# Attention in groups of two head pairs, with the transposes of the next group ahead of the scores of this one, on one Trainium2 core

## The chip, the cores and the metric

The kernel runs on one core of a Trainium2 chip. A core has engines that work side by side, each through its own list of instructions, in order: TensorE (PE in the profile; its weight loads are PEld), VectorE (DVE), ScalarE (ACT), GpSimd (POOL) and SyncE (SP), which here only issues transfers. 16 DMA engines move data between the chip's memory (HBM), the on-chip SBUF and PSUM, the small memory into which matmuls write. The metric is the device time of one execution in microseconds (us), as the median of several runs.

## The reference

Two stages follow each other. In the first, attention for B = 8 batches, H = 8 heads, S = 576 positions and D = 64, with two kinds of mask:

```
rel        = pos[:, None] - pos[None, :]
mask_plain = (rel >= 0) & (rel < 32)                       # heads 0 to 3
mask_dil   = (rel >= 0) & (rel < 128) & (rel % 4 == 0)     # heads 4 to 7
scores = where(mask, (q @ k.T) / sqrt(D), -1e9)
attn   = softmax(scores);   attn_out = attn @ v
```

In the second, the heads of a position are put side by side, so that x has 8 x 576 = 4608 rows of 8 x 64 = 512, and a feed-forward layer follows:

```
x = attn_out.transpose(0, 2, 1, 3).reshape(4608, 512)
h = x @ w_in             # 512 x 2048
g = h * sigmoid(h)
out = g @ w_out          # 2048 x 512
```

Inputs and output are float32.

## The kernel before, in words

**Set-up.** GpSimd builds the two masks as 128 x 512 tiles (L70 to L106), and its DMA queue then loads both weight matrices and casts them to bf16 on the way (L112, L113). Both masks reach at most 127 positions back, so a tile of 128 keys meets only the queries of its own tile and of the next one, 256 in all.

**A batch (loop at L180).** 576 positions are four tiles of 128 and a tail of 64. q and k are loaded by SP's queue and v by GpSimd's, a tile at a time (L184 to L195), then cast to bf16 on DVE into qb, kb and vb (L199 to L210). vb has two extra columns of ones per head, so that the matmul with v also gives the sum of the softmax. The load tiles qn, kn, vn and the cast tiles qb, kb, vb each have two buffers.

**A head pair (loop at L216), four to a batch.** Two heads fill the 128 partitions together:

1. Five PE transposes bring q of the pair into a PSUM tile `tpsq`, five bring k into `tpsk` (L227). DVE copies the first to qTp (L233), ACT the second to kTp (L235). qTp and kTp have two fixed buffers, used in turn. The trace calls both PSUM tiles tps, and the buffers of kTp kTp_307 and kTp_308.
2. For each of five key tiles j: two score matmuls (L241, L248), one for each head of the pair, into a PSUM tile sps; exp on ACT into Ej (L258); then DVE multiplies Ej by the mask in place (L259).
3. For each of the two heads: nine PV matmuls into the PSUM tile O_all (L274, L283, L291), a copy to SBUF, ost, on ACT (L301), then on DVE the reciprocal of the sums (L304) and the normalising product into xstage (L305, L312).

After the fourth pair SP issues two transfers of the batch's xstage to the DRAM tile x_sc (L321, L328).

**Buffers.** [...]transposes of q and of k one bank each (`T_psum`, one buffer for each), scores 2 buffers of two banks each (`S_psum`), PV results 2 buffers (`O_psum`). Ej has three buffers for each j. 

**Feed-forward (L139 to L174).** Nine blocks of 512 positions. Each loads x_sc with a DMA transpose (L142, SP), then one PE pass of 64 matmuls makes h (L149), with the sigmoid on ACT (L157) and the product on DVE (L158), and one more pass of 64 matmuls makes the output (L164), which ACT copies out of PSUM (L172) and SP stores (L174).

**What sets the order.** A tile scheduler puts the instructions of each engine in a list when the kernel is built. It gives priority by the order in which the program writes the operations, takes what it thinks ready by its own estimates of duration, and adds semaphore waits where an operation needs another's data or a buffer that is still in use. On the chip each engine goes through its list in order: an instruction that waits holds everything behind it on that engine.

The lines where a batch starts its pairs and fetches its buffers are short:

```
for hp in range(H // 2):
    ...
    qTc = qTp[hp % 2]
    kTc = kTp[hp % 2]
```

Of the kernel before, what the change touches and what calls it, by code (L numbers as in the profile page):

```python
# [9 lines left out]
ACT = mybir.ActivationFunctionType  # L10
ALU = mybir.AluOpType

NEG_BIAS = -3.0e4

PROBE = {"phase2": True, "scores": True, "pv": True, "norm": True, "xsc_write": True, "transposes": True}


@with_exitstack
def kernel(
# [9 lines left out]
    nc = tc.nc  # L29
    B, H, S, D = q.shape  # L30
# [3 lines left out]
    scale = 1.0 / math.sqrt(D)  # L34
# [3 lines left out]
    P = 128  # L38
    f32 = mybir.dt.float32
    bf16 = mybir.dt.bfloat16  # L40

    n_full_c = S // P
    tail = S - n_full_c * P
    n_qt = n_full_c + (1 if tail > 0 else 0)
    QT_W = (n_qt + 1) * P
# [9 lines left out]
    qkT_sb = cx1.enter_context(tc.tile_pool(name="qkT_sb", bufs=1))  # L55
    epool = cx1.enter_context(tc.tile_pool(name="e_pool", bufs=3))
    xst = cx1.enter_context(tc.tile_pool(name="xstage", bufs=2))
    rpool = cx1.enter_context(tc.tile_pool(name="r_pool", bufs=2))
    opool = cx1.enter_context(tc.tile_pool(name="o_pool", bufs=2))
    T_psum = cx1.enter_context(tc.tile_pool(name="T_psum", bufs=1, space=bass.MemoryType.PSUM))  # L60
    S_psum = cx1.enter_context(tc.tile_pool(name="S_psum", bufs=2, space=bass.MemoryType.PSUM))
    O_psum = cx1.enter_context(tc.tile_pool(name="O_psum", bufs=2, space=bass.MemoryType.PSUM))
# [37 lines left out]
    mask_pair = []  # L100
# [11 lines left out]
    nc.gpsimd.dma_start(out=w_in_bf, in_=moe_w_in.rearrange("(o p) f -> p o f", p=P))  # L112
    nc.gpsimd.dma_start(out=w_out_bf, in_=moe_w_out.rearrange("(o p) f -> p o f", p=P))  # L113

    qTp = [qkT_sb.tile([P, QT_W], bf16, name=f"qTp{i}") for i in range(2)]
    kTp = [qkT_sb.tile([P, S], bf16, name=f"kTp{i}") for i in range(2)]
    for t in qTp:
        nc.vector.memset(t[:, S:QT_W], 0.0)

    TB = 512  # L120
    n_blk = n_tok // TB
    n_nblk = d_ff // P
# [54 lines left out]
        moe_block_span(p * TB, TB)  # L177

    blocks_done = 0
    for b in range(B):  # L180
        qn = ld_nat.tile([P, n_qt, H, D], f32, tag="qn")
        kn = ld_nat.tile([P, n_qt, H, D], f32, tag="kn")
        vn = ld_nat.tile([P, n_qt, H, D], f32, tag="vn")
# [24 lines left out]
                out=vb[0:tail, n_full_c, :, 0:D], in_=vn[0:tail, n_full_c, :, :]  # L208
            )
        nc.vector.memset(vb[:, :, :, D : D + 2], 1.0)  # L210

        xstage = xst.tile([P, n_qt, H, D], bf16, tag="xstage")
        if not (PROBE["scores"] and PROBE["pv"] and PROBE["norm"]):
            nc.vector.memset(xstage[:, :, :, :], 0.0)

        for hp in range(H // 2):  # L216
            hA = 2 * hp
            mtile = mask_pair[0] if hA < H // 2 else mask_pair[1]

            qTc = qTp[hp % 2]  # L220
            kTc = kTp[hp % 2]
            if PROBE["transposes"]:
                for src, dstT, tagT in ((qb, qTc, "tpsq"), (kb, kTc, "tpsk")):
                    tps = T_psum.tile([P, S], bf16, tag=tagT)
                    for c in range(n_qt):
                        tn = P if c < n_full_c else tail
                        nc.tensor.transpose(  # L227
                            tps[:, c * P : c * P + tn],
                            src[0:tn, c, hA : hA + 2, :],
                            ident_bf[0:tn, 0:tn],  # L230
                        )
                    if src is qb:
                        nc.vector.tensor_copy(out=dstT[:, 0:S], in_=tps[:, 0:S])  # L233
                    else:
                        nc.scalar.copy(out=dstT[:, 0:S], in_=tps[:, 0:S])  # L235

            E = []
            for j in (range(n_qt) if PROBE["scores"] else ()):
                kn_j = P if j < n_full_c else tail
                sps = S_psum.tile([P, 8 * P], f32, tag="sps2")  # L240
                nc.tensor.matmul(  # L241
                    sps[0:kn_j, 0 : 2 * P],
                    lhsT=kTc[0:D, P * j : P * j + kn_j],
                    rhs=qTc[0:D, P * j : P * j + 2 * P],
                    start=True,
                    stop=True,
                )
                nc.tensor.matmul(  # L248
                    sps[0:kn_j, 4 * P : 6 * P],
                    lhsT=kTc[D : 2 * D, P * j : P * j + kn_j],  # L250
                    rhs=qTc[D : 2 * D, P * j : P * j + 2 * P],
                    start=True,
                    stop=True,
                )
                Ej = epool.tile([P, 4 * P], bf16, tag=f"E{j}")
                sps_view = sps[0:kn_j, :].rearrange("k (a b) -> k a b", b=4 * P)[:, :, 0 : 2 * P]
                e_view = Ej[0:kn_j, :].rearrange("k (a b) -> k a b", b=2 * P)
                nc.scalar.activation(out=e_view, in_=sps_view, func=ACT.Exp, scale=scale)  # L258
                nc.vector.tensor_tensor(  # L259
                    out=Ej[0:kn_j, :], in0=Ej[0:kn_j, :], in1=mtile[0:kn_j, :], op=ALU.mult  # L260
                )
                E.append((Ej, kn_j))

            for hh in (range(2) if (PROBE["pv"] and E) else ()):
                h = hA + hh
                oh = 2 * P * hh
                O_all = O_psum.tile([P, n_qt * (D + 2)], f32, tag="Oall")
                pv_order = ([n_qt - 1] + list(range(n_qt - 1))) if tail else list(range(n_qt))
                for i in pv_order:
                    qn_i = P  # L270
                    oreg = O_all[:, (D + 2) * i : (D + 2) * (i + 1)]
                    if i == 0:
                        Ej, kn_j = E[0]
                        nc.tensor.matmul(  # L274
                            oreg[0:qn_i, :],
                            lhsT=Ej[0:kn_j, oh : oh + qn_i],
                            rhs=vb[0:kn_j, 0, h, :],
                            start=True,
                            stop=True,
                        )  # L280
                    else:
                        Ep, kn_p = E[i - 1]
                        nc.tensor.matmul(  # L283
                            oreg[0:qn_i, :],
                            lhsT=Ep[0:kn_p, oh + P : oh + P + qn_i],
                            rhs=vb[0:kn_p, i - 1, h, :],
                            start=True,
                            stop=False,
                        )
                        Ej, kn_j = E[i]  # L290
                        nc.tensor.matmul(  # L291
                            oreg[0:qn_i, :],
                            lhsT=Ej[0:kn_j, oh : oh + qn_i],
                            rhs=vb[0:kn_j, i, h, :],
                            start=False,
                            stop=True,
                        )
                if not PROBE["norm"]:
                    continue
                ost = opool.tile([P, n_qt * (D + 2)], f32, tag="ost")  # L300
                nc.scalar.copy(out=ost[:, :], in_=O_all[:, :])  # L301
                rec = rpool.tile([P, n_qt, 1], f32, tag="rec")
                sview = ost[:, :].rearrange("p (c e) -> p c e", e=D + 2)
                nc.vector.reciprocal(out=rec[:, :, :], in_=sview[:, :, D : D + 1])  # L304
                nc.vector.tensor_tensor(  # L305
                    out=xstage[:, 0:n_full_c, h, :],
                    in0=sview[:, 0:n_full_c, 0:D],
                    in1=rec[:, 0:n_full_c, :].to_broadcast([P, n_full_c, D]),
                    op=ALU.mult,
                )  # L310
                if tail:
                    nc.vector.tensor_tensor(  # L312
                        out=xstage[0:tail, n_full_c : n_qt, h, :],
                        in0=sview[0:tail, n_full_c : n_qt, 0:D],
                        in1=rec[0:tail, n_full_c : n_qt, :].to_broadcast(
                            [tail, n_qt - n_full_c, D]
                        ),
                        op=ALU.mult,
                    )
        if PROBE["xsc_write"]:  # L320
            nc.sync.dma_start(  # L321
                out=x_sc[b * S : b * S + n_full_c * P, :].rearrange(
                    "(c p) (hh d) -> p c hh d", p=P, d=D
                ),
                in_=xstage[:, 0:n_full_c, :, :],
            )
            if tail:
                nc.sync.dma_start(  # L328
                    out=x_sc[b * S + n_full_c * P : (b + 1) * S, :].rearrange(
                        "p (hh d) -> p hh d", d=D  # L330
                    ),
                    in_=xstage[0:tail, n_full_c, :, :],
                )

    cx1.close()
    open_phase2_pools()
# [39 lines left out]
```

## Time and profile before

| | |
|---|---|
| median of 6 runs | 481.65 us (478.57 to 484.37) |
| span of the profiled execution | 483.7 us |
| busy over the span: PE, DVE, ACT, POOL | 398.3, 248.7, 240.6, 59.6 us |
| from 0 to 73.0 us: PE, DVE, ACT busy | 21.1, 21.5, 18.3 us; DMA moves 197 GB/s |
| from 73.0 to 230.4 us (attention): PE, DVE, ACT busy | 127.5, 126.4, 113.7 us of 157.4; 150 GB/s |
| from 230.4 to 483.7 us (feed-forward): PE, DVE, ACT busy | 249.7, 100.9, 108.6 us of 253.3; 55 GB/s |
| one exp of a key tile (ACT, L258), x160 | 597 ns |
| one mask product (DVE, L259), x160 | 413 to 416 ns |
| one ost copy (ACT, L301), x64 | 435 ns |
| one transpose (PE, L227), x320 | 287 to 291 ns |
| one v load issue (POOL, L187), x32 | 1018 ns |
| x_sc writes, from issue to landing, x8 | 3.3 us |

The shares of busy time over the whole span are a mean of stages that differ, so the table gives three stages. A group of the profile names line, engine, operation, tile written <- tiles read, their shape and type, the number of instructions, then the busy time and the mean duration of one, and the idle time of that engine just before these instructions with what ended most of it. A PE instruction counts as busy while it is in flight, and matmuls overlap, so a busy PE need not be at its peak. Idle time matters only on the chain of work that sets the end.

### The profile page before, as it was taken

How to read it: one execution, taken by the hardware profiler on the slowest of the kernel's cores; microseconds unless marked ns; L12 is line 12 of the kernel's file. 1: busy time of each engine (PE TensorE's matmuls, PEld its weight loads, DVE VectorE, ACT ScalarE, POOL GpSimd, SP SyncE). 2: the span in 40 equal slices, each digit the busy share in tenths (PEclk: the TensorE clock that was granted, in tenths of full speed). 3: DMA queues.
4: the chain of work that ended last, by engine and by line, in shares of the span. 5: the costliest groups of instructions: out<-in, count | busy, mean ns of one | idle time of the engine just before them, and what ended most of it. 6: DMA issues, size and time to landing. Idle time of an engine off the chain costs nothing.

```text
span 483.7 us, 6568 instructions
## 1 busy us (share of the span) xinstructions
PE 398.3 (82%) x2368; PEld 195.8 (40%) x2368; DVE 248.7 (51%) x588; ACT 240.6 (50%) x440; POOL 59.6 (12%) x117
## 2 busy tenths in 40 slices
PE   1261326788778787898999999999999999999996
PEld 0130213445444444454444444444444444444442
DVE  2261319878878878776733517072442608063350
ACT  1170217667767776876734426162533526163441
POOL 9920404404030400000000000000000000000000
PEclk9999999999999999999999999999999999999999
DMA  9999998998969891152121120303121030300101
GB/s 185 202 203 208 206 174 199 196 223 193 225 143 186 189 184 51 32 103 34 50 74 57 33 97 10 100 23 87 45 65 66 22 98 13 98 34 34 54 14 73
DMA packets 110208, 51.81 MB, mean 107 GB/s; under 512 B 96096, under 2 KB 102752, under 8 KB 110176
## 3 DMA queue, kind: packets, MB, share of 16 engines
q1 hardware_dynamic: 104640, 37.76, 36.3%
q0 software_dynamic: 5536, 13.63, 13.4%
q8 instruction: 18, 0.29, 0.2%
q14 instruction: 14, 0.11, 0.1%
HBM read 36.70 MB, written 14.16 MB: 105 GB/s over the span
## 4 chain that ended last, share of the span: by engine, by line
PE 56%; ACT 2%; DVE 1%; issue 0%; ACTq 0%; DVEq 0%
PE hps L149 26%; PE yps L164 26%; ACT Ej L258 2%; PE tps L227 1%; PE sps L241 1%; PE O_all L291 1%; ACT ost L301 1%; PE O_all L283 1%; DVE Ej L259 0%; PE O_all L274 0%; PE sps L248 0%; DVE rec L304 0%; DVE xstage L305 0%; ACT kTp_307 L235 0%; ACT ob L172 0%
## 5 line engine op out<-in xcount | busy, mean ns | idle before, releaser
L158 DVE TENSOR_TENSOR gT<-hps,sg 128x512 bf16<-128x512 f32 x144 | 99.5, 692 | 136.3 <-ACT sg L157 136.3
L149 PE MATMUL hps<-xT,w_in_bf 128*128 128x512 bf16 x576 | 128.4, 384 | 0.7 <-ACT Ej L258 0.7
L164 PE MATMUL yps<-w_out_bf,gT 128*128 128x512 bf16 x576 | 125.8, 379 | 0.0
L157 ACT ACTIVATE sg<-hps 128x512 f32<-128x512 f32 x144 | 85.9, 597 | 37.8 <-PE hps L149 37.8
L258 ACT ACTIVATE Ej<-sps 128x512 bf16<-128x512 f32 (+1 forms) x160 | 89.0, 597 | 9.4 <-PE sps L248 8.4
L149 PEld LDWEIGHTS <-w_in_bf 128*128 128x128 bf16 x576 | 56.9, 99 | 69.4 <-issue 3.1
L164 PEld LDWEIGHTS <-gT 128*128 128x128 bf16 x576 | 56.3, 98 | 68.0
L172 ACT COPY ob<-yps 128x512 f32<-128x512 f32 x36 | 21.1, 585 | 103.5 <-PE yps L164 103.5
L301 ACT COPY ost<-O_all 128x330 f32<-128x330 f32 x64 | 27.8, 435 | 58.7 <-PE O_all L291 23.4
L283 PE MATMUL O_all<-vb,Ej 128*128 128x66 bf16 x256 | 40.1, 244 | 17.8 <-DVE vb L205 13.2
L227 PE MATMUL tps<-ident_bf,kb 128*128 128x128 bf16 (+1 forms) x160 | 26.9, 287 | 29.5 <-DVE kb L200 11.6
L187 POOL DMA_DIRECT2D vn<-in_v_dram x32 | 32.3, 1018 | 104.9 <-DVE vb L207 57.8
L291 PE MATMUL O_all<-vb,Ej 128*128 128x66 bf16 (+1 forms) x256 | 42.9, 243 | 0.2
L241 PE MATMUL sps<-qTp_305,kTp_307 64*128 64x256 bf16 (+1 forms) x80 | 28.2, 394 | 17.0 <-ACT Ej L258 14.5
L283 PEld LDWEIGHTS <-Ej 128*128 128x128 bf16 x256 | 27.1, 126 | 23.4 <-issue 15.4
L227 PE MATMUL tps<-ident_bf,qb 128*128 128x128 bf16 (+1 forms) x160 | 26.0, 291 | 12.2 <-DVE qb L200 9.9
L259 DVE TENSOR_TENSOR Ej<-Ej,mask_pair_298 128x512 bf16<-128x512 bf16 (+1 forms) x80 | 31.6, 416 | 6.0 <-ACT Ej L258 4.5
L259 DVE TENSOR_TENSOR Ej<-Ej,mask_pair_295 128x512 bf16<-128x512 bf16 (+1 forms) x80 | 30.2, 413 | 8.1 <-ACT Ej L258 7.9
L227 PEld LDWEIGHTS <-kb 128*128 128x128 bf16 (+1 forms) x160 | 15.8, 121 | 41.7 <-issue 24.7
L241 PE MATMUL sps<-qTp_306,kTp_308 64*128 64x256 bf16 (+1 forms) x80 | 28.5, 390 | 4.5 <-ACT Ej L258 3.0
L291 PEld LDWEIGHTS <-Ej 128*128 128x128 bf16 (+1 forms) x256 | 29.1, 125 | 6.0 <-issue 0.5
L248 PE MATMUL sps<-qTp_306,kTp_308 64*128 64x256 bf16 (+1 forms) x80 | 29.1, 400 | 0.0
(47 smaller groups left out, 255.6 us busy)
## 6 DMA issues: line engine op xcount, KB each, us to landing
out_dram<-ob SPq DMA_DIRECT2D x36, 256.0 KB, 2.0
qn<-in_q_dram SPq DMA_DIRECT2D x32, 256.0 KB, 5.2
kn<-in_k_dram SPq DMA_DIRECT2D x32, 256.0 KB, 5.4
vn<-in_v_dram POOLq DMA_DIRECT2D x32, 256.0 KB, 7.4
x_sc<-xstage SPq DMA_DIRECT2D x8, 512.0 KB, 3.3
w_in_bf<-in_moe_w_in_dram POOLq DMA_DIRECT2D x1, 2048.0 KB, 16.3
w_out_bf<-in_moe_w_out_dram POOLq DMA_DIRECT2D x1, 2048.0 KB, 28.0
qn<-in_q_dram SPq DMA_DIRECT2D x8, 128.0 KB, 5.2
```

Of the source, the lines that this page charges most:

```text
L149: nc.tensor.matmul(hps[:, 0:tb], lhsT=w_in_bf[:, j, ni * P : (ni + 1) * P], rhs=xT[:, j, 0:tb], start=(j == 0), stop=(j == n_ftile - 1),)
L157: nc.scalar.activation(out=sg[:, 0:tb], in_=hps[:, 0:tb], func=ACT.Sigmoid)
L158: nc.vector.tensor_tensor(out=gT[:, ni, 0:tb], in0=hps[:, 0:tb], in1=sg[:, 0:tb], op=ALU.mult)
L164: nc.tensor.matmul(yps[:, :], lhsT=gT[:, ni, c * P : (c + 1) * P], rhs=w_out_bf[:, ni, :], start=(ni == 0), stop=(ni == n_nblk - 1),)
L187: eng.dma_start(out=dst[:, c, :, :], in_=src[b, :, c * P : (c + 1) * P, :].rearrange("hh p d -> p hh d"),)
L227: nc.tensor.transpose(tps[:, c * P : c * P + tn], src[0:tn, c, hA : hA + 2, :], ident_bf[0:tn, 0:tn],)
L241: nc.tensor.matmul(sps[0:kn_j, 0 : 2 * P], lhsT=kTc[0:D, P * j : P * j + kn_j], rhs=qTc[0:D, P * j : P * j + 2 * P], start=True, stop=True,)
L258: nc.scalar.activation(out=e_view, in_=sps_view, func=ACT.Exp, scale=scale)
L259: nc.vector.tensor_tensor(out=Ej[0:kn_j, :], in0=Ej[0:kn_j, :], in1=mtile[0:kn_j, :], op=ALU.mult)
L283: nc.tensor.matmul(oreg[0:qn_i, :], lhsT=Ep[0:kn_p, oh + P : oh + P + qn_i], rhs=vb[0:kn_p, i - 1, h, :], start=True, stop=False,)
L291: nc.tensor.matmul(oreg[0:qn_i, :], lhsT=Ej[0:kn_j, oh : oh + qn_i], rhs=vb[0:kn_j, i, h, :], start=False, stop=True,)
L301: nc.scalar.copy(out=ost[:, :], in_=O_all[:, :])
```

## The change

The four pairs of a batch are no longer a loop inside the batch. All 32 pairs of the 8 batches form one list, and the list is worked through in groups of two (`GR = 2`). The body of the old loop becomes functions: `ensure_batch` (loads and casts, at the first use of a batch), `stage_a` (the transposes of a pair and the copies to qTp and kTp), `stage_b_score_tile` (one key tile: scores, exp, mask), `stage_b_pv` (PV and normalising) and `write_batch`. For each group the program now writes first the transposes of the next group, which may belong to the next batch, then the score tiles of the two pairs in turns (j = 0 of the first, j = 0 of the second, j = 1 of the first and so on), and then the PV of both pairs. It is meant to give the engines work of another pair or batch while one pair waits.

qTp and kTp get four buffers each, since up to four pairs hold theirs at once. The write to x_sc goes from SP's queue to GpSimd's. `GB` isn't used, and the new switch in `PROBE` is on. The bodies of the functions, and everything from the feed-forward stage on, are as before.

```diff
-    qTp = [qkT_sb.tile([P, QT_W], bf16, name=f"qTp{i}") for i in range(2)]
-    kTp = [qkT_sb.tile([P, S], bf16, name=f"kTp{i}") for i in range(2)]
+    qTp = [qkT_sb.tile([P, QT_W], bf16, name=f"qTp{i}") for i in range(4)]
+    kTp = [qkT_sb.tile([P, S], bf16, name=f"kTp{i}") for i in range(4)]
     for t in qTp:
         nc.vector.memset(t[:, S:QT_W], 0.0)
...
-    for b in range(B):
+    batch_data = {}
+
+    def ensure_batch(b):
+        if b in batch_data:
+            return
         qn = ld_nat.tile([P, n_qt, H, D], f32, tag="qn")
...
+        batch_data[b] = (qb, kb, vb, xstage)
+
+    def stage_a(b, hp):
...
+        idx = b * (H // 2) + hp
+        qTc = qTp[idx % 4]
+        kTc = kTp[idx % 4]
...
+    def stage_b_score_tile(b, hp, qTc, kTc, j, E):
...
+    def stage_b_pv(b, hp, E):
...
+    def write_batch(b):
...
-            nc.sync.dma_start(
+        nc.gpsimd.dma_start(
...
+    npairs_per_batch = H // 2
+    pairs = [(bb, hp) for bb in range(B) for hp in range(npairs_per_batch)]
+    GR = 2
+    aheads = {}
+    def emit_stage_a(i):
+        if i < len(pairs) and i not in aheads:
+            nb, nhp = pairs[i]
+            ensure_batch(nb)
+            aheads[i] = stage_a(nb, nhp)
+    for i in range(min(GR, len(pairs))):
+        emit_stage_a(i)
+    for g0 in range(0, len(pairs), GR):
+        group = list(range(g0, min(g0 + GR, len(pairs))))
+        for i in group:
+            emit_stage_a(i + GR)
+        Es = {i: [] for i in group}
+        for j in (range(n_qt) if PROBE["scores"] else ()):
+            for i in group:
+                b, hp = pairs[i]
+                qTc, kTc = aheads[i]
+                stage_b_score_tile(b, hp, qTc, kTc, j, Es[i])
+        for i in group:
+            b, hp = pairs[i]
+            stage_b_pv(b, hp, Es[i])
+            if hp == npairs_per_batch - 1:
+                write_batch(b)
```

## The prediction

> **What bounds the kernel now.** I read the slices of the span first. They split the run into a loading stage, an attention stage and a feed-forward stage that starts near slice 19 (a slice is 12.1 us).
>
> ```profile
> ## 2 busy tenths in 40 slices
> PE   1261326788778787898999999999999999999996
> DVE  2261319878878878776733517072442608063350
> ACT  1170217667767776876734426162533526163441
> DMA  9999998998969891152121120303121030300101
> ```
>
> From slice 19 PE is full. In slices 6 to 18 no engine is: DVE shows 8, ACT 7, PE 8, DMA 9 until slice 14. Then the chain of work that ended last, in order of time:
>
> ```profile
> 230.45 14.81 PE hps L149 x61
> 245.26 13.81 PE yps L164 x64
> ...
> 466.27 13.83 PE yps L164 x64
> 480.17 0.58 ACT ob L172
> ```
>
> From 230.45 on, 18 passes of 13.81 us follow each other without a gap. The change leaves them alone, so the time moves only with the moment at which PE becomes solid, 230.45 here. Third, the attention stage cut at the moments when a batch's output was written (SP issued those writes at 78.1, 101.4 and so on):
>
> ```profile
> core 0: us, PE busy (x) PEld busy (x) DVE busy (x) ACT busy (x) POOL busy (x), PEclk, DMA share, GB/s
> 78.10:101.40 23.30, 18.01 (x152) 10.62 (x152) 19.37 (x59) 15.06 (x31) 9.30 (x9) 1.00 1.02 212
> 101.40:121.70 20.30, 17.22 (x145) 9.50 (x145) 16.84 (x55) 14.94 (x30) 5.07 (x5) 1.00 0.93 208
> 121.70:146.60 24.90, 18.73 (x159) 10.93 (x159) 19.82 (x58) 17.44 (x35) 4.68 (x5) 1.00 0.88 170
> ...
> 213.60:231.70 18.10, 15.73 (x119) 8.28 (x118) 12.12 (x42) 13.01 (x26) 0.00 (x0) 1.00 0.40 70
> sum 153.60, PE 125.59 PEld 70.04 DVE 122.54 ACT 110.19 POOL 24.13; mean PE 17.94 PEld 10.01 DVE 17.51 ACT 15.74 POOL 3.45
> ```
>
> A batch takes 153.6/7 = 21.9 us, of which DVE works 17.5 and waits 4.4, and ACT works 15.7. So latency between engines costs about a fifth, and DVE sets the floor. The DVE timeline shows where the stage starts:
>
> ```profile
> 60.38 0.18 DVE L304 RECIPROCAL rec<-ost 128x5 f32<-128x5 f32 x1
> 71.03 1.23 DVE L200 CAST qb<-qn 128x2048 bf16<-128x2048 f32 x1 [10.47 <-DMA qn<-in_q_dram]
> ```
>
> The cast of batch 2's q waits 10.47 us for its load and holds all of DVE's queue. And the ACT timeline shows what a pair waits for:
>
> ```profile
> 128.69 0.62 ACT L235 COPY kTp_307<-tps 128x576 bf16<-128x576 bf16 x1
> 130.31 0.64 ACT L235 COPY kTp_308<-tps 128x576 bf16<-128x576 bf16 x1 [1.00 <-PE tps L227]
> 130.85 0.43 ACT L301 COPY ost<-O_all 128x330 f32<-128x330 f32 x1
> ```
>
> Two k copies can't follow each other: there is one PSUM buffer for k transposes, so the second set of transposes starts when the first copy has ended, and ACT idles 1.00 us. The ost copy is behind both in ACT's queue.
>
> **What the Trainium skill says.** "Trainium Architecture — The Big Picture", section "Inside one NeuronCore": each engine has its own instruction stream, and they meet only in semaphores. The trace agrees: ost at 130.85 is held by the copy ahead of it. "Perfetto Trace Analysis", "Optimization Strategy": a gap that repeats can mean that SBUF or PSUM ran out for the next tile. That is the 1.00 us above. "DMA: Bandwidth & Descriptors", "Issuing engines are not separate DMA queues": moving a transfer to another queue saves issue time alone, since all share 16 DMA engines. And "SBUF — State Buffer", "SBUF: two separate sides": DMAs of GpSimd get their descriptors from that engine, which a DVE copy between SBUF operands can lock out. In this trace the issue of a v load takes 1.02 us on POOL beside a DVE that is 80% busy, so the harm is small.
>
> **The change part by part.** *Removed and added work.* Matmuls, exps, mask products, casts and copies stay the same in number and shape; two 0.14 us memsets are added while DVE waits for the first load. So DVE still owes 17.5 us a batch (17.9 when I add up the spacings in its timeline: 20 masks at 0.345, three casts at 1.12 with tails at 0.33, eight heads of 0.47 plus a reciprocal of 0.17, four qT at 0.37). Only the order can gain.
>
> *The start.* Up to 71.03 the loads are issued in the same order, and the order of instructions on DVE has batch 2's q cast at the same place (its 46th). So DVE again waits until 71.03. Ahead of it the interleaving has masked only two tiles of the third pair (before: all five), since the fourth pair's scores hold one of the two score buffers; three masks, 1.0 us, are owed later. They are in my sum.
>
> *One batch in the new order.* I laid the three queues of one batch beside each other with durations from the trace (exp 0.55 apart and 0.60 long, ost 0.33/0.43, kT 0.53/0.62, a PV head 0.65, five transposes 0.75, a score pair 0.40). DVE then waits five times. (1) and (2) 0.37 each, when the second and the fourth head's reciprocal wait for their ost copies, between the casts. (3) 1.23 at the second pair's qT: its transposes stand on PE behind four k transposes of the third pair, and those wait for kT1, the copy that ends the serial k chain on ACT. Behind qT stand eight masks; for those waits PV, and for PV the next ost. (4) 0.92 at the next group's first reciprocal, whose ost is behind kT3 and an exp. (5) 0.97 at the fourth qT, whose transposes are split around two PV heads. Sum 3.86, so a batch takes 17.9 + 3.9 = 21.8 us against 21.9. The lookahead does not remove the waits, because the PSUM buffer for transposes stays single, and four pairs' transposes now come in one bunch. ACT needs 16.1 and idles 5.7, so it is not the bound.
>
> *What is gained at the two ends.* From 71.03: 10.0 us of DVE work to the end of batch 0, 2.4 of masks, 1.4 of waits: 84.9. Batch 1's cycle lacks one cast (1.12): 105.5. Five cycles of 21.8: batch 7's last group starts its heads at 214.5. It has no casts and no transposes; ten exps and six ost copies on ACT, a stall of 0.5 and one of 0.45 bring the last exp to 221, and then four PV heads with ost copies between them make PE solid 9.6 us after the start, at 224.1. That is 6.4 before 230.45. The gain is this: at a batch's end the next batch's first two pairs are nearly masked, where they were hardly begun.
>
> *Allowance.* My layout has no jitter; the batches before spread from 20.3 to 24.9. I take 0.35 us a batch, 2.4 in all, for what it misses (bounds 0 and 1.2). Net -4.0.
>
> *Queues.* x writes move from SP to POOL. On SP, q and k loads stood behind them (batch 7's last k chunks were issued at 191.4, after batch 5's write); now they are paced by casts. After 73 us DVE waits for a load once more in this stage, 0.9 us before a q cast, so I cost this at under 1 us a run and inside the allowance: the masks and casts hide the rest. On POOL a v load of batch b+3 now stands behind batch b's write. It has two batches, 43 us, to land, and takes 7.4: nothing. Sixteen more issues at about 1 us lie beside DVE. Four qT and kT buffers instead of two: before, no wait of any length came from them: nothing. Batch 7's write is needed only by feed-forward block 7, 190 us later.
>
> **The rivals.** *A, small gain (chance 0.50):* 481.65 - 4 = 477.5. For it: the layout; against: a third of the gain is at the end, where I assume that PE finds its operands. *B, waits vanish (0.15):* if two interleaved pairs hide the chain, DVE runs at 90% and a batch takes 17.5/0.9 = 19.5. Over 6.5 batches that is -15, with the end -18 at most: 464 to 467. Loads allow it: 3.54 MB a batch at 200 GB/s is 17.7. Against it: waits (3) to (5) come from in-order PE and one PSUM buffer. *C, the gain is eaten (0.15):* waits 0.9 a batch longer than laid out take all 6.4: 481. *D, slower (0.20):* the bunch of transposes, four PV heads in a row between scores, and exps held by late score buffers, cost 1.8 a batch: 7 x 1.8 - 6.4 = +6, so 488. For it: PE is in order and the new order puts whole heads between scores, and each exp needs a score that is 0.40 + 0.60 us around the loop with only two buffers; ACT's spacing of 0.55 has no slack there.
>
> **How the numbers follow.** A is likeliest, so 477.5. Within 1% is 476.8 to 486.5. Half of A and a little more lies below 476.8 together with B: 0.30 + 0.15 = 0.45. A's rest and C: 0.36. D's upper part and a tail: 0.19. The range from 467 takes most of B and to 488 half of D.
>
> **What would show it.** PE solid at 225 to 227; 18 passes of 13.81 unchanged. Batches 21.8 to 22.3 apart, DVE about 80% busy. The 10.5 us wait for batch 2's q at 71 stays. After it, DVE idle of about 1 us each before qT copies (for PE tps) and before a reciprocal. ACT waits before kT copies. No DMA wait of DVE later, even with POOL's writes. Wrong would make it: batches under 20.5 (B), exps with long waits on sps and batches over 23 (D), vb casts waiting for v loads, or the first stall being gone or longer.

## The result and the profile after

The changed kernel takes 477.83 us (median of 20 runs, 471.14 to 480.30), and the kernel before, run beside it, 483.89 us (40 runs, 478.57 to 486.09). The ratio is 0.984, with a 95% interval of 0.980 to 0.988. This ratio and those below leave out slow runs (over 1.5% above the fastest of their kernel: here nine of the 20 and three of the 40); the medians of all runs give 0.987. Runs of one kernel spread over 7 to 9 us, so below I compare spacings inside the profiles first and times second.

The slices of the span after, in the view that the prediction opened with:

```profile
## 2 busy tenths in 40 slices
PE   1261226887878788888999999999999999999996
DVE  2251208888778797876815335070633518062450
ACT  1161135877768686777616345271634526162441
DMA  9999999999998930250131211203021120301101
```

The stages are the same three, and PE is full from slice 19 on in both kernels: slices of 12 us are too coarse for a gain of 6. The chain of work that ended last says when PE becomes solid:

```profile
217.54 2.09 ACT Ej L267 x4
219.64 0.60 ACT Ej L267
220.29 0.59 PE hps L150
...
224.07 4.54 PE hps L150 x18
228.62 0.21 PE yps L165
228.83 9.50 PE hps L150 x44
238.33 13.60 PE yps L165 x63
251.93 13.81 PE hps L150 x64
```

From 224.07 PE runs through, 6.4 us earlier than 230.45 before; the passes of 13.81 us are unchanged. The span is 7.1 us shorter (476.6 against 483.7): the other 0.7 is in the first pass, 14.0 us against 14.8. The attention stage, cut at the moments when x was written, now by GpSimd:

```profile
core 0: us, PE busy (x) PEld busy (x) DVE busy (x) ACT busy (x) POOL busy (x), PEclk, DMA share, GB/s
82.58:104.09 21.51, 18.02 (x152) 10.29 (x151) 17.56 (x57) 16.70 (x35) 11.11 (x11) 1.00 1.14 227
104.09:125.56 21.47, 17.72 (x152) 10.42 (x152) 17.50 (x56) 15.89 (x34) 7.67 (x9) 1.00 1.12 215
...
189.99:211.46 21.47, 17.71 (x152) 10.42 (x152) 17.51 (x56) 15.90 (x34) 2.76 (x2) 1.00 0.34 78
211.46:224.07 12.61, 10.75 (x95) 6.02 (x95) 9.23 (x34) 8.75 (x20) 1.33 (x2) 1.00 0.14 48
```

A full batch takes 21.47 to 21.51 us, where the full batches before took 20.3 to 25.0. DVE is busy 17.5 us of it. The same 17.5 in the prediction is a mean that holds the short last interval, so it can't be set against this. The six full batches together, first before and then after, in the columns of the view above:

```profile
78.11:213.57 135.46, 109.84 (x919) 61.76 (x918) 110.38 (x335) 97.17 (x192) 24.12 (x24) 1.00 0.77 159
```

```profile
82.58:211.46 128.88, 106.61 (x912) 62.40 (x911) 105.10 (x332) 96.20 (x195) 38.32 (x37) 1.00 0.82 162
```

For each batch that is 18.4 us of busy DVE in 22.6 before and 17.5 in 21.5 after. The instructions are nearly the same in number (335 and 332) and in mean duration, and busy time counts overlapping instructions once, so DVE's instructions overlap more. One likely reason: mask products that waited singly for their exp, 0.42 us each, now often stand in rows (eight take 2.75 us). No run tests it.

On DVE's own timeline the wait for batch 2's q is still there, and one batch shows exactly five further waits:

```profile
71.15 1.23 DVE L205 CAST qb<-qn 128x2048 bf16<-128x2048 f32 x1 [11.14 <-DMA qn<-in_q_dram]
...
150.49 0.19 DVE L317 RECIPROCAL rec<-ost 128x5 f32<-128x5 f32 x1 [0.47 <-ACT ost L314]
153.62 0.19 DVE L317 RECIPROCAL rec<-ost 128x5 f32<-128x5 f32 x1 [0.47 <-ACT ost L314]
158.50 0.46 DVE L238 COPY qTp_306<-tps 128x576 bf16<-128x576 bf16 x1 [0.92 <-PE tps L232]
163.17 0.19 DVE L317 RECIPROCAL rec<-ost 128x5 f32<-128x5 f32 x1 [0.84 <-ACT ost L314]
165.35 0.46 DVE L238 COPY qTp_308<-tps 128x576 bf16<-128x576 bf16 x1 [1.13 <-PE tps L232]
```

**Where the 6.4 us come from.** Three stretches, each from the moments of the x writes. Up to batch 0's write: 82.58 against 78.11, so 4.5 us later, because the next pairs' work is now mixed in. From batch 0's write to batch 6's: 128.9 us (82.58 to 211.46) against 135.5 (78.11 to 213.57), so 6.6 are gained, 1.1 a batch. From batch 6's write to PE solid: 12.6 against 16.9 (213.57 to 230.45), so 4.3 are gained. Together -6.4. The two ends nearly cancel: the gain is in the six full batches.

### The profile page after: what moved, and what is told of

It is laid out like the page before. It is cut to its first block, busy times and chain, and to the rows that moved or that the text cites. A ratio compares the mean times of both kernels' runs of the same rounds, so it can differ in the third digit from the quotient of the medians.

```text
span 476.6 us, 6580 instructions
## 1 busy us (share of the span) xinstructions
PE 394.0 (83%) x2368; PEld 197.1 (41%) x2368; DVE 244.2 (51%) x590; ACT 237.9 (50%) x440; POOL 75.5 (16%) x133
## 4 chain that ended last, share of the span: by engine, by line
PE 55%; ACT 1%; issue 0%; ACTq 0%
PE hps L150 26%; PE yps L165 26%; ACT Ej L267 1%; PE O_all L304 1%; PE O_all L296 1%; PE O_all L287 0%; PE sps_t L248 0%; ACT ost L314 0%; PE sps_t L255 0%; PE tps L232 0%; ACT ob L173 0%; ACTq L173 0%
## 5 line engine op out<-in xcount | busy, mean ns | idle before, releaser
L267 ACT ACTIVATE Ej<-sps_t 128x512 bf16<-128x512 f32 (+1 forms) x160 | 90.0, 603 | 13.9 <-PE sps_t L255 12.7
L232 PE MATMUL tps<-ident_bf,kb 128*128 128x128 bf16 (+1 forms) x160 | 25.5, 290 | 21.4 <-DVE kb L205 11.2
L192 POOL DMA_DIRECT2D vn<-in_v_dram x32 | 29.4, 928 | 46.9 <-DVE vb L215 20.4
L269 DVE TENSOR_TENSOR Ej<-Ej,mask_pair_295 128x512 bf16<-128x512 bf16 (+1 forms) x80 | 29.8, 404 | 4.9 <-ACT Ej L267 4.6
L269 DVE TENSOR_TENSOR Ej<-Ej,mask_pair_298 128x512 bf16<-128x512 bf16 (+1 forms) x80 | 29.0, 414 | 2.0 <-ACT Ej L267 1.8
L318 DVE TENSOR_TENSOR xstage<-ost,rec 128x256 bf16<-128x256 f32 x64 | 26.4, 413 | 0.2
L232 PEld LDWEIGHTS <-qb 128*128 128x128 bf16 (+1 forms) x160 | 16.3, 129 | 21.6 <-DVE qb L205 9.9
L338 POOL DMA_DIRECT2D x_sc<-xstage x8 | 6.2, 778 | 105.9 <-DVE xstage L325 105.9
```

The source lines that it names most:

```text
L192: eng.dma_start(out=dst[:, c, :, :], in_=src[b, :, c * P : (c + 1) * P, :].rearrange("hh p d -> p hh d"),)
L232: nc.tensor.transpose(tps[:, c * P : c * P + tn], src[0:tn, c, hA : hA + 2, :], ident_bf[0:tn, 0:tn],)
L269: nc.vector.tensor_tensor(out=Ej[0:kn_j, :], in0=Ej[0:kn_j, :], in1=mtile[0:kn_j, :], op=ALU.mult)
L318: nc.vector.tensor_tensor(out=xstage[:, 0:n_full_c, h, :], in0=sview[:, 0:n_full_c, 0:D], in1=rec[:, 0:n_full_c, :].to_broadcast([P, n_ful ...
```

## Experiments

Each is an edit of the changed kernel unless it says otherwise. The scheduler places all instructions anew for each, so an edit of the program's order is an edit of many positions.

To compare runs whose batch 2 q arrives at different times I use two figures: the spacing of batches, which is the time from batch 1's write of x to batch 6's divided by 5, and the rest, which is the span minus the moment at which DVE's wait for that q ends. Before: 22.4 us and 412.7 (483.7 - 71.0). After: 21.5 and 405.4 (476.6 - 71.15). Two figures in the expectations, 23.4 us for no lookahead and 22.9 for groups of one, are single batches.

### The x write back on SP

```diff
-        nc.gpsimd.dma_start(out=x_sc[...], in_=xstage[...])   # both
+        nc.sync.dma_start(out=x_sc[...], in_=xstage[...])
```

> The changed kernel with the two writes of x back on SP's queue; all else stays. My theory (the gain is the overlap across batches, the queue is worth nothing): 477.5 us, within 1.5 us of the changed kernel, a batch every 21.5 us, PE solid at 224 to 225. Rival (part of the gain is that q and k loads no longer stand behind x writes on SP): 480 to 483 us, with new waits of DVE for q or k loads after 73 us.

Measured: 478.94 us, ratio 0.987 (0.983 to 0.990), spacing 21.5, rest 406.0 (477.9 - 71.86). The queue is worth nothing here, and DVE has no wait for a load after 72 us, which the rival would need. The later runs show where that ends.

### No lookahead

```diff
-            emit_stage_a(i + GR)
+            emit_stage_a(i)
```

The two calls ahead of the loop go too.

> The changed kernel in which each group's transposes are written in the program ahead of its own scores and not one group earlier; pairs are still interleaved. My theory (the gain is that the next batch's first pairs run ahead at a batch's end): the first group of a batch begins later, PE solid at 229 to 231, 482 to 484 us. Rival (the interleaving alone does it, since the scheduler brings ready transposes forward by itself): 476 to 479 us.

Measured: 487.82 us, ratio 1.004 (1.001 to 1.006), spacing 22.8, rest 416.1 (479.1 - 63.02). Without lookahead the change is a small loss, larger than the 482 to 484 us that I expected. One batch of it, in DVE's waits:

```profile
DVE rec L317 <- ACT ost L314: 3.4, 3, 1.6
...
DVE Ej L269 <- ACT Ej L267: 0.9, 4, 0.3
DVE qTp L238 <- PE tps L232: 0.5, 1, 0.5
```

The columns are the total, the number of waits and the longest. The new wait is in the first line: single waits of 1.29 and 1.59 us for the first ost of a group, where the changed kernel has none above 0.84.

### Lookahead inside a batch only

```diff
         for i in group:
-            emit_stage_a(i + GR)
+            emit_stage_a(i)
+        for i in group:
+            if i + GR < len(pairs) and pairs[i + GR][0] == pairs[i][0]:
+                emit_stage_a(i + GR)
```

> The changed kernel with the transposes one group ahead only inside a batch: the first group of each batch has its transposes written just before its own scores. My theory (what the lookahead gives is the start of the next batch while this one ends): a batch takes about 23.4 us as it does without any lookahead, 486 to 488 us. Rival (lookahead inside a batch does half of it): a batch takes 22.4 us, 481 to 483 us. Third (the boundary is worth nothing): 21.5 us, 477 us.

Measured: 487.82 us, ratio 1.006 (1.002 to 1.009), spacing 23.0, rest 416.0 (480.5 - 64.46). It is as slow as no lookahead at all. So what the lookahead gives comes from the boundary between two batches.

### Groups of one pair

```diff
-    GR = 2
+    GR = 1
```

> The changed kernel with groups of one pair: the transposes stay one group, now one pair, ahead, the scores of two pairs are no longer interleaved. My theory (overlap across batches carries the gain): 477 to 479 us, with PE solid at 224 to 226. Rival (interleaving hides the wait of one pair behind the other and carries the gain): 482 to 485 us, waits of DVE above 4.4 us a batch as in the kernel before.

Measured: 486.81 us, ratio 0.998 (0.993 to 1.003), spacing 23.2, rest 415.0 (485.5 - 70.5). My theory missed here: it took the boundary alone to be enough. Three things were changed at once, though: the interleaving, the depth of the lookahead, which is now one pair, and the place of PV, which now follows each pair instead of every second. The next run parts the interleaving from the other two.

### Groups of two, not interleaved

```diff
-        for j in (range(n_qt) if PROBE["scores"] else ()):
-            for i in group:
+        for i in group:
+            for j in (range(n_qt) if PROBE["scores"] else ()):
```

> The changed kernel with groups of two and the transposes of the next group ahead, but all five key tiles of the first pair ahead of the five of the second. My theory, after the run with groups of one (22.9 us a batch): lookahead and interleaving are both needed, 22.5 to 23.3 us a batch, 484 to 487 us. Rival (groups of one lost only because its lookahead is one pair deep): 21.5 us a batch, 477 to 479 us.

Measured: 473.05 us, ratio 0.977 (0.966 to 0.987), spacing 22.0, rest 404.3 (467.8 - 63.48). My theory missed again. A batch is 0.5 us longer than with interleaving, and the total is no worse: the interval holds the changed kernel's 0.984, and the rest is 1.1 us shorter. Interleaving the score tiles is worth nothing in the end. What groups of one had lost is the lookahead two pairs deep, or the PV of two pairs together; no run parts these two.

### Two PSUM buffers for k transposes

```diff
-                tps = T_psum.tile([P, S], bf16, tag=tagT)
+                tps = T_all[:, t0 : t0 + S]   # t0: q 0; k 640 or 1280, in turns
```

T_all is a tile of 2048 columns in the two banks that held the two transposes.

> The changed kernel with three transpose buffers of 640 columns in the two PSUM banks that held two: one for q, two for k. My theory (the wait of 0.92 us at the second pair's qT in each batch comes from k transposes that wait for the single buffer, and PE is in order): this wait vanishes, cycle 20.5 us instead of 21.5, PE solid at 217 to 218, 471 us. Rival (what DVE then waits for is the ost chain on ACT, which takes the wait over): cycle 21.2 to 21.5 us, 476 to 478 us.

Measured: 485.36 us, ratio 0.990 (0.987 to 0.993), spacing 22.3, rest 413.3 (483.3 - 70.0). The median beside it of the kernel before is 485.04, so over all runs nothing is left of the gain. DVE's waits of one batch, first here and then in the changed kernel:

```profile
DVE rec L320 <- ACT ost L317: 3.7, 5, 1.3
DVE qTp L241 <- PE T_all L235: 0.3, 1, 0.3
```

```profile
DVE rec L317 <- ACT ost L314: 1.8, 3, 0.8
DVE qTp_308 L238 <- PE tps L232: 1.1, 1, 1.1
DVE qTp_306 L238 <- PE tps L232: 0.9, 1, 0.9
```

The wait before qT copies falls from 2.0 to 0.3 us, so the buffer was its cause or a large part of it. But the waits for ost rise from 1.8 to 3.7, and the batch gets longer, not shorter. The rival had the mechanism and was too mild. The scheduler also gave another order, and the three buffers now share two banks, so how much of the loss belongs to the buffer itself isn't settled.

### No ost copy

```diff
-            ost = opool.tile([P, n_qt * (D + 2)], f32, tag="ost")
-            nc.scalar.copy(out=ost[:, :], in_=O_all[:, :])
+            ost = O_all
```

> The changed kernel without the ost copy on ACT: reciprocal and normalising product read O_all in PSUM. My theory (the copy on ACT is what heads wait for): the waits of 0.47, 0.47 and 0.84 us a batch before reciprocals vanish and ACT has 3.5 us a batch less to do[...]. A batch takes 20.5 to 21.5 us, 471 to 477.5 us. Rival (DVE is the floor and pays more than it saves, and PV tiles stay occupied longer): 22 us or more a batch, above 480 us.

Measured: 484.08 us, ratio 1.002 (0.999 to 1.005), spacing 24.1. Two groups of DVE and the waits of one batch:

```profile
L317 DVE TENSOR_TENSOR xstage<-O_all,rec 128x256 bf16<-128x256 f32 x8 | 3.3, 410 | 0.0
...
L316 DVE RECIPROCAL rec<-O_all 128x5 f32<-128x5 f32 x8 | 1.6, 195 | 5.1 <-PE O_all L304 5.1
```

```profile
DVE rec L316 <- PE O_all L304: 5.1, 8, 1.6
...
PEld L296 <- DVE xstage L324: 0.7, 1, 0.7
```

Reading PSUM costs DVE almost nothing: the product takes 410 ns from PSUM and 411 from SBUF, the reciprocal 195 against 182. So one half of the rival (DVE pays) is wrong, though its outcome came. All eight heads of a batch now wait, 5.1 us in all against 1.8: taking the copy off ACT did not shorten what a head waits for. The rival's other half, that PV's two PSUM buffers stay occupied longer, has one sign in this batch: the weight load of one PV waits 0.7 us for the product that reads such a buffer last (the second line), which the changed kernel's batch doesn't have. That is at most 0.7 of the 2.6 us by which a batch is longer; the cause of the rest stays open.

### The weights in pieces, later

```diff
-    nc.gpsimd.dma_start(out=w_in_bf, in_=moe_w_in.rearrange(...))
-    nc.gpsimd.dma_start(out=w_out_bf, in_=moe_w_out.rearrange(...))
...
+        # in ensure_batch, behind the loads: halves of w_in for b = 2, 3; quarters of w_out for b = 4 to 7
+        for wt, wv, o0, o1 in w_parts.get(b, ()):
+            nc.gpsimd.dma_start(out=wt[:, o0:o1, :], in_=wv[:, o0:o1, :])
```

> The changed kernel with the two weight loads cut into pieces and issued behind the v loads of batches 2 to 7, in place of one piece each ahead of all v loads. My theory (the DVE wait that ends at 71 us is batch 2's q load standing behind 8.4 MB of weights in the DMA engines, and everything later is anchored to it): the first v cast comes near 30 us instead of 54.7, the wait at 71 us is gone, a batch takes 21.5 us or, where DMA is the limit, up to 23, and PE is solid at 195 to 205 us: 447 to 458 us. Rival (the loads are late because DMA is full in any case; weights then delay later batches by as much): 470 to 478 us.

Measured: 463.56 us, ratio 0.960 (0.952 to 0.967). The wait at 71 us is gone, and the first v cast comes at 32.45 instead of 54.67. It beat the rival and missed my figure, for a reason that DVE's timeline shows:

```profile
107.12 1.23 DVE L208 CAST qb<-qn 128x2048 bf16<-128x2048 f32 x1 [3.50 <-DMA qn<-in_q_dram]
115.75 1.23 DVE L208 CAST kb<-kn 128x2048 bf16<-128x2048 f32 x1 [6.01 <-DMA kn<-in_k_dram]
```

The scheduler issued the quarters of w_out as soon as it could, the last at 103.49, ahead of loads that were needed. So a part of the delay, these 9.5 us of waits, had only moved.

### The weights last, in both kernels

In the changed kernel, then in the kernel before, the two loads at the start go, and in their place stand:

```diff
+    # in write_batch, behind the x write: w_in for b = 4, w_out for b = 5
+            nc.gpsimd.tensor_copy(out=wt[0:1, 0, 0:1], in_=xstage[0:1, 0, H - 1, 0:1])
+            nc.gpsimd.dma_start(out=wt, in_=wv)
```

The copied element is overwritten by the load; it only makes the load wait for the batch.

> The changed kernel with both weight loads held back: w_in behind the output of batch 4, w_out behind that of batch 5 (a copy of one element from the batch's output into the weight tile makes each wait). My theory (everything is anchored to the loads at the start, and with the weights later in pieces DVE still waited 9.5 us for q and k of one batch because the pieces came too early): no wait of DVE for loads above 5 us, batch 0 written at about 56.6 us as with the weights in pieces, then 21.5 us a batch, PE solid at 198 us, 452 us. Rival (DMA is the limit of the stage in any case, 4.1 MB a batch): 22.5 us or more a batch, 458 to 464 us.

> The kernel before with the same two weight loads held back in the same way. My theory (what the change gains is in the order of the pairs and is independent of the anchor at the start): 6 to 8 us above the changed kernel with weights held back, about 459 us, 21.9 to 22.5 us a batch. Rival (the change gains by the way the start is anchored): within 2 us of the changed kernel with weights held back.

Measured: the changed kernel 454.29 us, ratio 0.939 (0.933 to 0.945), first x write at 56.59, spacing 21.5 (79.48 to 187.02). My figure of 452 was close. The kernel before: 477.48 us, ratio 0.987 (0.979 to 0.995), spacing 25.4. That is neither 459 nor within 2 us of the other. DVE's waits in its attention stage:

```profile
DVE kb L208 <- DMA kn<-in_k_dram: 14.2, 3, 7.0
DVE Ej L267 <- ACT Ej L266: 11.3, 27, 1.2
DVE rec L312 <- ACT ost L309: 6.1, 15, 0.6
```

DVE waits 14.2 us for k. SP's timeline shows what those loads stood behind:

```profile
144.84 0.39 SPq L329 DMA_DIRECT2D x_sc<-xstage  x1
145.33 0.52 SPq L336 DMA_DIRECT2D x_sc<-xstage  x1
145.90 15.66 SPq L195 DMA_DIRECT2D kn<-in_k_dram  x4
```

SP issues in order, and its x write waits for the batch's last head; batch 6's k loads come only then, and the cast that needs them waits 5.76 us, until 164.68. But something else comes at the same moment, on GpSimd's queue:

```profile
145.96 0.76 POOL L121 DMA_DIRECT2D w_in_bf<-in_moe_w_in_dram  x1 [0.30 <-POOL w_in_bf L120]
```

The weights themselves, held back to this point, share the DMA engines with these k loads: issuing four of them took 15.66 us, where it took 3.28 for batch 4. The longest wait, 7.0 us for batch 7's k, falls beside the w_out load in the same way (both issued from 173.7 on). So late loads and the weights act together here.

### The kernel before with the weights last and x on GpSimd

The edit is that of the last run and of the first, together, on the kernel before.

> The kernel before with the weights held back, as in the run that took 477.5 us, and with the two writes of x on GpSimd's queue. My theory (in that run DVE waited 14.2 us for k loads that stood in SP's queue behind an x write; with that gone the old order of the pairs shows its own cost): no wait of DVE for loads above 3 us, 21.9 to 22.5 us a batch, 459 to 463 us, so 5 to 9 us above the changed kernel with weights held back (454.3). Rival (the loads' order in the queues is not it; the old order of the pairs itself is much worse once weights don't hold the start): 470 us or more. Third (with both the gain of the change vanishes): 453 to 456 us.

Measured: 461.72 us, ratio 0.952 (0.949 to 0.954), spacing 22.4. DVE's waits:

```profile
DVE rec L312 <- ACT ost L309: 14.1, 31, 1.3
DVE Ej L267 <- ACT Ej L266: 6.8, 25, 0.7
DVE qTp L241 <- PE tps L235: 3.5, 7, 0.5
```

The k waits are gone, and the spacing is that of the kernel before, 22.4. With this early start the changed order, its four buffers included, is still 7.4 us better (461.72 - 454.29), against 6.1 behind the old start. So the order's gain doesn't come from the way the start is anchored. The queue of the x write, worth nothing in the changed kernel behind the old start, is worth 15.8 us (477.48 - 461.72) here. The k loads of batches 6 and 7 are now issued from 115.72 and 137.75 on, ahead of the w_in load at 148.30, so the 15.8 holds the meeting with the weights too; no run parts the two.

### Casting in the transfer

```diff
+            # batches 2 to 7: four buffers of qb, kb, vb, no qn, kn, vn and no casts on DVE
+            for src, dst in ((q, qb), (k, kb), (v, vb)):
+                nc.gpsimd.dma_start(out=dst[:, c, :, 0:D], in_=src[b, :, c * P : (c + 1) * P, :]...)
```

The weights stand in eight pieces behind batch 7's loads. "DMA: Bandwidth & Descriptors", section "SWDGE vs HWDGE vs iDMA", of the Trainium skill says that only GpSimd's transfers can change the type on the way, which is why the q and k loads move there. No run here tries another queue.

> The changed kernel in which q, k and v of batches 2 to 7 are loaded by GpSimd's queue straight into bf16 tiles (four buffers), so that DVE casts only two batches, and the weight loads stand behind batch 7's loads. My theory (DVE sets the floor): DVE has 17.5 - 4.8 = 12.7 us a batch, the limit becomes ACT (15.9 us and its waits) or DMA, 19 to 20 us a batch, PE solid near 185 us, 438 to 444 us. Rival (15 load issues of 0.93 us a batch on GpSimd and the x writes behind them hold the loads up, or the chain of latencies stays): 21.5 us or more a batch, 452 us or more.

Measured: 440.90 us, ratio 0.912 (0.906 to 0.918), the best version. Its attention stage, by batch:

```profile
93.63:113.10 19.47, 17.72 (x152) 10.29 (x152) 15.08 (x49) 16.41 (x33) 14.65 (x19) 1.00 1.57 126
113.10:132.26 19.16, 17.72 (x152) 10.33 (x152) 14.90 (x49) 15.94 (x32) 13.97 (x17) 1.00 1.54 124
```

The third number of busy time is DVE's: it falls from 17.5 to 15.0 us, not to the 12.7 expected, and a batch from 21.5 to 19.4. A likely part of the difference: products that wait singly for their exp show their whole 0.42 us, where products in a row are spaced 0.345. GpSimd is busy 14 us of a batch with issues. Of DVE and ACT, ACT is now the fuller, with 15.9 to 16.4 us; PE is in flight for 17.7 us, as in the changed kernel.

## Why the prediction was right

**The bound and the start.** PE solid was the right moment to follow, and the wait for batch 2's q stayed: 71.15 against the 71.03 that I took over. That it came at the same time is luck in part, since it comes at 63.0 to 64.5 in other runs (last section). The runs with later weights (454.29 us with the weights last) confirm that the rest hangs on it.

**The waits of a batch.** I laid out 0.37, 0.37, 1.23, 0.92 and 0.97, 3.86 in sum; the trace has 0.47, 0.47, 0.92, 0.84 and 1.13, 3.83, at the same instructions in the same order. A batch takes 21.47 against 21.8, because DVE owes 17.6 a batch (21.47 - 3.83), not 17.9. Rival B thus falls as argued, and C and D with it: the waits are not longer and the batch is not.

**The comparison with before.** The prediction used 153.6/7 = 21.9 us for a batch before. That mean holds the last interval of 18.1, which has no casts. The six full ones average 22.6 (135.5/6), so the cycle gains 1.1 us a batch, where the prediction's words credit it with 0.1 and put the gain at the two ends. This step of the reasoning was wrong. The layout itself already held the gain: it has 129.6 us from batch 0's end to batch 6's (214.5 - 84.9), 5.9 less than the 135.5 before, and the trace has 128.9. DVE's 17.5 us a batch before has the same fault; a full batch had 18.4, and waits of 4.2 us against 4.0 after. So most of the gain is in busy time, which the prediction took as fixed. The total was right because it was added up from spacings, in which overlap is contained, and not from this comparison.

**The two ends.** Predicted were 84.9 for the end of batch 0, 105.5, 214.5, and 9.6 us from there to PE solid. The x writes came at 82.58, 104.09 and 211.46, and the tail took 12.6. The sum, 224.1, met 224.07, but with two errors of 3 us that cancel: batch 6's output came 3.0 us earlier than laid out, 2.3 of it already at batch 0, and the tail took 3.0 longer. That the sum met is luck to this extent. Batch 1's cycle wasn't shorter for the missing cast (21.51 us).

**The allowance.** The 2.4 us for jitter weren't needed: the cycles agree within 0.05 us. Without it the forecast was -6.4, and the measured medians differ by -6.1. That 477.5 met 477.83 so closely is partly luck: the forecast change was 4.15 us, the measured one 6.06, and the median before was 481.65 then and 483.89 in the larger sample.

**Edits costed at nothing or nearly.** The x write on GpSimd: confirmed by putting it back (0.987 against 0.984, intervals overlapping), and DVE has no load wait after 72 us. But it was hidden, not free: with the weights last the same edit of the old order is worth 15.8 us. That another queue saves issue time alone, on which the prediction leaned, doesn't hold there: loads had stood in SP's order behind a write that waited for compute. The four qT and kT buffers were not tried alone.

**The reason given for the waits.** "The PSUM buffer for transposes stays single" named the cause of wait (3), or a large part of it: with two k buffers, qT waits fall from 2.0 to 0.3 us. "Perfetto Trace Analysis", section "Optimization Strategy", of the Trainium skill reads a repeated gap in the same way. What the prediction didn't say, and what I then expected, is wrong: removing the gap gains nothing, as ost waits grow by 1.9 us.

**Where the gain sits.** "At a batch's end the next batch's first two pairs are nearly masked": the run with lookahead inside a batch only loses everything, as this sentence needs. Groups of one, with one pair ahead and PV after each pair, gain nothing (0.998, interval 0.993 to 1.003). Interleaving, the other half of the change, isn't needed.

## What to carry to other kernels

Lay the in-order queues of one steady cycle beside each other with measured durations: it gave five waits to about 0.3 us each, which a sum of busy times can't. Busy time isn't fixed either: the same instructions kept DVE busy for 18.4 us a batch in one order and 17.5 in the other. Compare like with like, full cycles with full cycles, and first find what anchors the stage: the order of loads at the start was worth 23.5 us (477.83 - 454.29), the whole reordering 6 to 7. And an edit that is worth nothing behind one bound (the queue of a write) can be worth 16 us once that bound has gone. "Perfetto Trace Analysis", section "DMA Optimizations", of the Trainium skill says that it may make sense to give inputs and outputs separate issuing engines; here, with v still loaded on the queue that took the writes, this is worth 15.8 us in one setting, where loads would otherwise meet the weights, and nothing in the other.

## What the runs showed of the hardware

Batch 2's q arrives at one of two times. In the profiled runs of eight versions with weights ahead of v, DVE's wait for it ended at 70.0 to 71.9 us (before, after, x on SP, groups of one, two k buffers) or at 63.0 to 64.5 (no lookahead, lookahead inside a batch, not interleaved). Times of one such kernel spread over 3 to 10 us. In the five versions with later weights, where no load holds DVE at that place, they spread over 0.4 to 1.3 us (453.79 to 454.76, for one). A ninth version with weights ahead of v, the one without the ost copy, reaches this cast only at 76.08, without a wait, and its runs spread over 2.9 us. The profiled runs themselves agree: the three with the early arrival are 0 to 0.9 us above the shortest run of their kernel, the five with the late one 3.3 to 7.6 us. That the arrival makes the spread is likely from this; for the runs without a profile it isn't shown.

Loads that change the type keep the DMA engines busier for each byte counted: a share of 1.54 at 124 GB/s with casting, against 1.12 at 215 GB/s without. The trace counts the cast loads at their bf16 size (128 KB each, against 256 KB). Counted at float32, the first is about 215 GB/s too (an estimate: 4.1 MB a batch in 19.2 us, from the sizes of q, k, v and x), so the casting loads keep the engines about 1.4 times as busy.
